# Moving the down-projection weight gradient of a spectral-plus-MLP backward pass out of the MLP into a filler phase

## The chip, the cores and the metric

One core of a Trainium2 chip runs the whole program. The metric is device time in microseconds (us) of one execution. Before the change six executions gave 2395.0 to 2404.82 us, with a median of 2399.89.

## The reference

The reference computes a block and the gradients of all its inputs but B_x: sequence S = 2048, width D = 576, hidden width F = 4608, bfloat16.

```
mod = (silu(c) @ w_mod).reshape(6, D)          # sa, ca, ga, sb, cb, gb
h   = layernorm(x) * (1 + ca) + sa
x   = x + ga * irfft2(rfft2(h) * (w_r + 1j*w_i))
h   = layernorm(x) * (1 + cb) + sb
x   = x + gb * ((h @ w_gate) * (h @ w_up)) @ w_down
out, vjp = jax.vjp(block, A_x, w_r, w_i, w_gate, w_up, w_down, c, w_mod)
return (out, *vjp(grad_out))
```

With hh = (h @ w_gate) * (h @ w_up) and dO = grad_out * gb, the gradient of w_down is hh^T @ dO, a [4608, 576] product over all 2048 rows. It is the product that the change moves.

## The kernel before

The program is written with a tile framework: the code names tiles in pools with a number of buffers, and a list scheduler fixes the order of the instructions on each engine ahead of time, from the order of the code, the data and the free buffers. Each engine then runs its own list in order, and waits on semaphores where it must. A transfer is issued by an engine's queue: most by SP, a few by ACT and POOL.

The 2048 rows are held as 16 blocks of 128 rows (NB = 16; HB = 8 is half of them). The stages, in order:

1. Tables of sines and cosines (build_tables: Fd, FdB, FdT, CF, SF, PT, K), stored to DRAM for the backward pass.
2. The rows of dO = grad_out * gb (tile dO_b), transposed into dOT (pt_b), 16 blocks. Then the spectral weights: load_w_xlayout loads Wn (2048 x 289 twice) and transposes it to Wx (pt_w). Then LayerNorm 1 by rows into h1T.
3. rfft2 as matmuls (ps_d, ps_s1, ps_s2), cmul (product with Wx), irfft2u (ps_s2i, transposes pt_z, ps_s1i, then for each row block ps_y). Each ps_y goes to cons_fwd: ya, x2, LayerNorm 2, h2, and a transpose into h2T, which is stored as one transfer.
4. mlp_phase: two halves (hf = 0, 1) of 1024 rows, and in each nine chunks of 512 columns of F. A chunk loads its weights, computes ps_g, ps_u, ps_d, the products hhT, dgT and duT, the output sum ps_o, the transposes hh_c, dg_c and du_c, the input gradient ps_h, and the weight gradients ps_dwd (line 618, from hh_c and dO_h) and ps_dw (line 628). dw_out stores the weight gradients of half 0 as fp32 partial sums (dWd_p, dWg_p, dWu_p); in half 1 it loads them (dw_f), adds and writes the result (dw_bf). The he rows follow each half (he_row: xn_b and ya_b are loaded by POOL, lb_dx, dya_b); those of half 1 stand after the MLP.
5. Backward transform: Wx again, rfft2 of dyAT, cmul, then the gradient of the spectral weights (cmul_conj_f32 into gWx, store_w_natural with transposes pt_gw into gWn), then irfft2u with cons_bwd for each ps_y: LayerNorm backward on DVE, lb_dx on POOL, and the column sums acc_sa and acc_ca added up on POOL.
6. finals: column sums ps_cs, the row gradients gathered in gm, the gradient of w_mod as five products ow, and that of c.

Of the kernel before, what the change touches and what calls it, by code (L numbers as in the profile page):

```python
# [7 lines left out]
ACT = mybir.ActivationFunctionType  # L8
# [17 lines left out]
class K:  # L26

    def __init__(self, ctx, tc, dbg=None):
        self.ctx = ctx
        self.tc = tc  # L30
        self.nc = tc.nc
        self.dbg = dbg or {}
        self.evac_i = 0
# [80 lines left out]
    def build_tables(self, es=None):  # L114
        nc, tc, ctx = self.nc, self.tc, self.ctx
        self.tpool = (es or ctx).enter_context(tc.tile_pool(name="tables", bufs=1))
# [3 lines left out]
        with tc.tile_pool(name="tgen", bufs=1) as gp, tc.tile_pool(name="tgen2", bufs=2) as gp2:  # L120
# [25 lines left out]
            self.FdB = tpb.tile([128, 5, 2, DF], BF16, name="FdB")  # L146
            nc.vector.tensor_copy(self.FdB[:], self.Fd[:])
            nc.vector.tensor_scalar(self.FdB[:, :, :, 0:1], self.Fd[:, :, :, 0:1], 0.5, None, op0=ALU.mult)
            nc.vector.tensor_scalar(self.FdB[:, :, :, DF - 1:DF], self.Fd[:, :, :, DF - 1:DF], 0.5, None, op0=ALU.mult)
            self.FdT = tpb.tile([128, 3, 2, D], BF16, name="FdT")  # L150
            self.FdTA = tp.tile([128, 3, 2, D], BF16, name="FdTA")
            di = gp.tile([128, D], I32, name="di")
            nc.gpsimd.iota(di[:], pattern=[[1, D]], base=0, channel_multiplier=0)
            d_row = gp.tile([128, D], FP32, name="d_row")
            nc.vector.tensor_copy(d_row[:], di[:])
            kci = gp.tile([128, 3], I32, name="kci")
            for kc, (k0, ksz) in enumerate(KCH):
                nc.gpsimd.iota(kci[:, kc:kc + 1], pattern=[[0, 1]], base=k0, channel_multiplier=1)
            k_col = gp.tile([128, 3], FP32, name="k_col")
            nc.vector.tensor_copy(k_col[:], kci[:])  # L160
            sc0 = gp.tile([128, 3], FP32, name="sc0")
            sc1 = gp.tile([128, 3], FP32, name="sc1")
            nc.vector.tensor_scalar(sc0[:], k_col[:], 0.0, -0.5, op0=ALU.is_equal, op1=ALU.mult)
            nc.vector.tensor_scalar(sc1[:], k_col[:], float(DF - 1), -0.5, op0=ALU.is_equal, op1=ALU.mult)
            nc.vector.tensor_tensor(sc0[:], sc0[:], sc1[:], op=ALU.add)
            nc.vector.tensor_scalar(sc0[:], sc0[:], 1.0, None, op0=ALU.add)
            for kc in range(3):
                idx = gp2.tile([128, D], FP32, tag="idx_fdt", name="idx_fdt")
                nc.vector.tensor_scalar(idx[:], d_row[:], k_col[:, kc:kc + 1], None, op0=ALU.mult)
                self.trig3(gp2, {"cos": self.FdT[:, kc, 0, :], "nsin": self.FdT[:, kc, 1, :]}, idx[:], D, [128, D])  # L170
                nc.vector.tensor_scalar(self.FdTA[:, kc, :, :], self.FdT[:, kc, :, :], sc0[:, kc:kc + 1], None, op0=ALU.mult)
# [11 lines left out]
            idx = gp.tile([128, NB, 128], FP32, name="idx_cf")  # L183
# [3 lines left out]
            self.PT = tp.tile([128, NB, 3, 128], BF16, name="PT")  # L187
            sri = gp.tile([128, NB, 128], I32, name="sri")
            nc.gpsimd.iota(sri[:], pattern=[[1, NB], [NB, 128]], base=0, channel_multiplier=0)
# [289 lines left out]
for _f in (transpose_b, ln_rows, phase0_mod, layernorm_fwd, transpose_sd, rfft2, irfft2u, load_w_xlayout, cmul):  # L479
    setattr(K, _f.__name__, _f)  # L480
# [591 lines left out]
```

## Time and profile before

| | |
|---|---|
| median of six executions | 2399.89 us (2395.0 to 2404.82) |
| the profiled execution's own time | 2402.17 us |
| its span in the profile | 2400.3 us |
| mean granted TensorE clock | 0.868 |
| busy: PE, DVE, ACT, POOL | 1854.4, 1161.5, 764.9, 284.8 us |
| DMA | 262.49 MB in 270574 packets |
| first and last ps_y, forward | 252.9, 328.3 us |
| first ps_g | 361.5 us |
| first and last ps_y, backward | 2234.8, 2319.5 us |

Busy time is a sum over stages. A stage is read by its own stretch: which engine is full in it, which waits, and for whom. In the rows that follow, a group's line gives engine, operation, tiles and shape, count, busy time and the mean of one in ns, then the idle time of the engine ahead of it and what ended that. Rows of the chain give the start in us, the length and what it was. In table rows of a transfer, the last number is the median time from issue to landing in us. L with a number is a line of the kernel before.

### The profile page before, as it was taken

What the parts mean: (1) busy time and instruction counts of PE and PEld (TensorE: products, weight loads), DVE (VectorE), ACT (ScalarE), POOL (GpSimd) and SP (SyncE); (2) the same over time, 40 slices, a digit from 0 to 9 for tenths busy, and PEclk for the clock granted to TensorE, in tenths of its full rate; (3) what the DMA queues carried; (4) which work ended last, traced back from release to release, by engine and by line L of the source; (5) the groups of instructions that cost most, each with busy time, mean ns of one, the idle gap of its engine ahead of it and who ended that gap; (6) DMA issues with size and microseconds to landing.
All of it is one profiled execution on the core that took longest, in us unless ns stands there. A gap on an engine that the chain in (4) does not pass through costs nothing. (4 is left out here: it accounts for less than half of the span.)

```text
span 2400.3 us, 31077 instructions
## 1 busy us (share of the span) xinstructions
PE 1854.4 (77%) x12125; PEld 1142.5 (48%) x12223; DVE 1161.5 (48%) x2125; ACT 764.9 (32%) x1189; POOL 284.8 (12%) x301
## 2 busy tenths in 40 slices
PE   2375749999999999996789999999999961824630
PEld 1253525656566656663446556556555630613420
DVE  7446642234333433342864444434444466294793
ACT  3467524232322332231322211211311310538422
POOL 1100340000000000001430000000000035000670
PEclk7587659999999999997899999999999985965655
DMA  3620373342234224219563253244243055111135
GB/s 121 225 76 41 126 268 84 89 118 76 64 97 116 51 70 118 79 60 299 167 195 77 75 144 92 79 125 106 71 119 99 29 185 195 53 41 40 52 116 137
DMA packets 270574, 262.49 MB, mean 109 GB/s; under 512 B 136806, under 2 KB 222694, under 8 KB 268764
## 3 DMA queue, kind: packets, MB, share of 16 engines
q1 hardware_dynamic: 261580, 237.05, 34.2%
q0 software_dynamic: 4640, 20.65, 2.7%
q10 hardware_dynamic: 4208, 2.81, 0.4%
q8 instruction: 95, 1.56, 0.3%
q14 instruction: 51, 0.42, 0.1%
HBM read 128.45 MB, written 101.33 MB: 96 GB/s over the span
## 5 line engine op out<-in xcount | busy, mean ns | idle before, releaser
L604 PE MATMUL ps_h<-wgT_c,dgT 128*128 128x288 bf16 x1152 | 297.3, 287 | 0.0
L606 PE MATMUL ps_h<-wuT_c,duT 128*128 128x288 bf16 x1152 | 294.5, 287 | 0.0
L628 PEld LDWEIGHTS <-h_h 128*128 128x128 bf16 (+1 forms) x1440 | 142.7, 102 | 224.0 <-issue 79.7
L561 ACT CAST gT<-ps_g 128x512 bf16<-128x512 f32 x144 | 84.4, 586 | 469.0 <-PE ps_g L551 414.4
L551 PE MATMUL ps_g<-h2T_h,wg_c 128*128 128x512 bf16 x683 | 177.0, 384 | 19.4 <-DMA h2T_h<-h2T_s 16.2
L554 PE MATMUL ps_u<-h2T_h,wu_c 128*128 128x512 bf16 x702 | 180.1, 383 | 7.5 <-DVE dw_bf L671 6.6
L628 PE MATMUL ps_dw<-dg_c,h_h 128*128 128x512 bf16 (+1 forms) x702 | 164.4, 390 | 27.0 <-DVE dw_bf L671 18.0
L594 PE MATMUL ps_o<-wd_c,hhT 128*128 128x288 bf16 x1152 | 172.6, 287 | 12.8 <-DVE hhT L575 12.2
L557 PE MATMUL ps_d<-dOT_h,wdT_c 128*128 128x512 bf16 x720 | 179.9, 381 | 3.4 <-DVE dw_bf L671 1.7
L628 PE MATMUL ps_dw<-du_c,h_h 128*128 128x512 bf16 (+1 forms) x702 | 165.6, 385 | 13.7 <-DVE dw_bf L671 8.0
L575 DVE TENSOR_TENSOR hhT<-gT,uT 128x512 bf16<-128x512 bf16 x144 | 62.3, 433 | 230.3 <-ACT uT L562 230.1
L711 ACT COPY dg_c<-pt 128x512 bf16<-128x512 bf16 x144 | 84.4, 586 | 238.1 <-DVE hh_c L710 238.1
L618 PE MATMUL ps_dwd<-dO_h,hh_c 128*128 128x288 bf16 x1152 | 144.4, 286 | 2.3 <-DVE dw_bf L671 2.3
L612 DVE TENSOR_TENSOR dh_acc<-dh_acc,ps_h 128x576 f32<-128x576 f32 x128 | 96.5, 754 | 96.6 <-PE ps_h L606 96.6
L526 POOL MEMSET wg_c<- 64x512 bf16 x18 | 9.3, 519 | 1083.5 <-PE ps_g L551 1003.1
L618 PEld LDWEIGHTS <-hh_c 128*128 128x128 bf16 x1152 | 112.7, 98 | 31.0 <-issue 2.6
L594 PEld LDWEIGHTS <-hhT 128*128 128x128 bf16 x1152 | 108.4, 98 | 37.0 <-DVE hhT L575 13.6
L606 PEld LDWEIGHTS <-duT 128*128 128x128 bf16 x1152 | 113.1, 98 | 25.5
L604 PEld LDWEIGHTS <-dgT 128*128 128x128 bf16 x1152 | 113.3, 98 | 24.7
L671 DVE TENSOR_TENSOR dw_bf<-dw_f,ps_dw 128x512 bf16<-128x512 f32 (+1 forms) x90 | 61.6, 685 | 118.7 <-DMA dw_f<-dWu_p 57.7
L551 PEld LDWEIGHTS <-wg_c 128*128 128x128 bf16 x720 | 69.8, 99 | 98.3 <-issue 15.1
L554 PEld LDWEIGHTS <-wu_c 128*128 128x128 bf16 x720 | 70.9, 99 | 94.6 <-issue 11.9
(362 smaller groups left out, 2965.2 us busy)
## 6 DMA issues: line engine op xcount, KB each, us to landing
wd_c<-in_B_w_down_dram SPq DMA_DIRECT2D x18, 576.0 KB, 4.2
dWd_p<-dw_f SPq DMA_DIRECT2D x36, 288.0 KB, 2.6
dw_f<-dWd_p SPq DMA_DIRECT2D x36, 288.0 KB, 3.3
wg_c<-in_B_w_gate_dram SPq DMA_DIRECT2D x18, 512.0 KB, 3.9
wu_c<-in_B_w_up_dram SPq DMA_DIRECT2D x18, 512.0 KB, 5.0
dWg_p<-dw_f SPq DMA_DIRECT2D x36, 256.0 KB, 2.0
dWu_p<-dw_f SPq DMA_DIRECT2D x36, 256.0 KB, 2.0
dw_f<-dWg_p SPq DMA_DIRECT2D x36, 256.0 KB, 2.8
```

The lines of the kernel that those rows point to most:

```text
L551: nc.tensor.matmul(ps_g[:], wg_c[:, kt, fs], h2T_h[:, kt, cs], start=(kt == 0), stop=(kt == 4))
L554: nc.tensor.matmul(ps_u[:], wu_c[:, kt, fs], h2T_h[:, kt, cs], start=(kt == 0), stop=(kt == 4))
L557: nc.tensor.matmul(ps_d[:], wdT_c[:, kt, fs], dOT_h[:, kt, cs], start=(kt == 0), stop=(kt == 4))
L561: nc.scalar.copy(gT[:], ps_g[:])
L575: nc.vector.tensor_tensor(hhT, v4(gT), v4(uT), op=ALU.mult)
L594: nc.tensor.matmul(ps_o[:, h, :288], (hhTs[ft][:, st, :] if USE_DMA_T else hhTs[ft][:, ss]), wd_c[:, ft, h * 288:(h + 1) * 288], start=(ft ...
L604: nc.tensor.matmul(ps_h[:, h, :288], (dgTs[ft][:, st, :] if USE_DMA_T else dgTs[ft][:, ss]), wgT_c[:, ft, h * 288:(h + 1) * 288], start=(f ...
L606: nc.tensor.matmul(ps_h[:, h, :288], (duTs[ft][:, st, :] if USE_DMA_T else duTs[ft][:, ss]), wuT_c[:, ft, h * 288:(h + 1) * 288], start=Fa ...
L612: nc.vector.tensor_tensor(da, da, ps_h[:, :, :288], op=ALU.add)
L618: nc.tensor.matmul(ps[:, h, :288], hh_c[:, bl, fs], dO_h[:, bl, h * 288:(h + 1) * 288], start=(bl == 0), stop=(bl == HB - 1))
L628: nc.tensor.matmul(ps[:dsz, :], h2_h[:, bl, kt * 128:kt * 128 + dsz], src_c[:, bl, :], start=(bl == 0), stop=(bl == HB - 1))
L711: nc.scalar.copy(dg_c[:, sb * 4:(sb + 1) * 4, fs], pt1[:, 4:8, :])
```

## The change

**The down-projection gradient.** With DEFER_DWD the MLP no longer computes ps_dwd. It stores hh_c to DRAM (hh_s), and after the code of the backward transform dwd_filler computes the gradient in 36 steps of 128 columns of F, each over all 2048 rows, so that there is no partial sum. Its instructions are laid by the scheduler between those of the backward transform, and behind them.

```diff
-                        for ft in range(4):
+                        if DEFER_DWD:
+                            nc.gpsimd.dma_start(scr["hh"][:, hf * HB:(hf + 1) * HB, f0:f0 + FC], hh_c[:])
+                        for ft in (range(0) if DEFER_DWD else range(4)):
                             fs = slice(ft * 128, (ft + 1) * 128)
                             ps = psAcc.tile([128, 2, 512], FP32, tag="acc", name="ps_dwd")
...
+def dwd_filler(self, pool, psum_pool, scr, out_6, dO_all):
+    nc = self.nc
+    for ft in range(F // 128):
+        hh_t = pool.tile([128, NB, 128], BF16, tag="hh_t", name="hh_t")
+        nc.gpsimd.dma_start(hh_t[:], scr["hh"][:, :, ft * 128:(ft + 1) * 128])
+        ps = psum_pool.tile([128, 2, 512], FP32, tag="fill", name="ps_fill")
+        for h in range(2):
+            for b in range(NB):
+                nc.tensor.matmul(ps[:, h, :288], hh_t[:, b, :], dO_all[:, b, h * 288:(h + 1) * 288],
+                                 start=(b == 0), stop=(b == NB - 1))
+        o = pool.tile([128, 2, 288], BF16, tag="dwd_o", name="dwd_o", bufs=1)
+        nc.scalar.copy(o[:], ps[:, :, :288])
+        nc.gpsimd.dma_start(out_6[ft * 128:(ft + 1) * 128, :].rearrange("p (h d) -> p h d", h=2), o[:])
...
+        if DEFER_DWD:
+            fp_ = es.enter_context(tc.tile_pool(name="fillp", bufs=2))
+            dO_all = fp_.tile([128, NB, D], BF16, name="dO_all", bufs=1)
+            nc.gpsimd.dma_start(dO_all[:], scr["dO"])
+            kb.dwd_filler(fp_, kb.psF, scr, out_6, dO_all)
```

On PE, in the first chunk of the MLP, the input gradient ps_h is followed before by ps_dwd (64 matmuls to a chunk):

```order
L604 MATMUL ps_h<-wgT_c,dgT 128x288
L606 LDWEIGHTS duT
L606 MATMUL ps_h<-wuT_c,duT 128x288
L618 LDWEIGHTS hh_c
L618 MATMUL ps_dwd<-dO_h,hh_c 128x288
```

and in the changed kernel, at the same place (its line numbers are its own):

```order
L628 MATMUL ps_h<-wgT_c,dgT 128x288
L630 LDWEIGHTS duT
L630 MATMUL ps_h<-wuT_c,duT 128x288
L654 LDWEIGHTS h_h
L654 MATMUL ps_dw<-dg_c,h_h 128x512
```

The gate's weight gradient ps_dw now follows ps_h at once.

On POOL, at the end of the MLP, the he rows of half 1 begin before with their loads, right behind the memsets of the last chunks:

```order
L526 MEMSET wg_c 64x512
L526 MEMSET wu_c 64x512
L535 MEMSET wdT_c 64x512 x2
L728 DMA xn_b<-xn_s 128x576
L730 DMA ya_b<-ya_s 128x576
L728 DMA xn_b<-xn_s 128x576
```

and now the last stores of hh_c, the load of dO_all and the first two loads of the filler stand ahead of them:

```order
L638 DMA hh_s<-hh_c 128x8x512
L817 MEMSET wdT_c 64x512
L638 DMA hh_s<-hh_c 128x8x512 x2
L1080 DMA dO_all<-dO_s 128x9216
L801 DMA hh_t<-hh_s 128x16x128 x2
L754 DMA xn_b<-xn_s 128x576
L756 DMA ya_b<-ya_s 128x576
```

So three large loads were put ahead of the rows on POOL's queue.

On POOL, at the end of the program, the list ends before with the column sums of cons_bwd and lb_dx:

```order
L692 TENSOR_TENSOR lb_dx<-lb_v,dx_b 128x576
L962 TENSOR_TENSOR acc_sa<-acc_sa,dh_20985 128x576
L965 TENSOR_TENSOR acc_ca<-acc_ca,pr 128x576
L692 TENSOR_TENSOR lb_dx<-lb_v,dx_b 128x576
L965 TENSOR_TENSOR acc_ca<-acc_ca,pr 128x576
L692 TENSOR_TENSOR lb_dx<-lb_v,dx_b 128x576 x2
```

and now with pairs of a filler load and a filler store, 17 loads behind the last lb_dx:

```order
L718 TENSOR_TENSOR lb_dx<-lb_v,dx_b 128x576
L809 DMA out_dram<-dwd_o 128x576
L801 DMA hh_t<-hh_s 128x16x128
L809 DMA out_dram<-dwd_o 128x576
L801 DMA hh_t<-hh_s 128x16x128
L809 DMA out_dram<-dwd_o 128x576
```

The sums acc_sa and acc_ca are gone from POOL, and the filler's transfers stand in the row phase and behind it. On PE the same list puts 784 of the filler's 1152 matmuls behind the last ps_y.

**The backward transform.** rfft2 of dyAT no longer waits for Wx, which is loaded behind it. irfft2u with cons_bwd stands ahead of cmul_conj_f32 and store_w_natural. The column sums acc_sa and acc_ca become two stores per row block (rows_sa, rows_ca), loaded again and summed by 64 matmuls with a vector of ones.

```diff
         kb.rfft2(dyAT, kb.FdB, G)
+        Wx = kb.load_w_xlayout(kb.stg, A_w_r, A_w_i)
         gX = kb.stg.tile([128, 2, NKH, 128], BF16, tag="stg", name="gX")
         kb.cmul(wk, gX, G, Wx, conj_b=True)
+        def cons_bwd(b, ps):
...
+            nc.sync.dma_start(scr["rows_sa"][:, b, :], dh1b[:])
...
+            nc.sync.dma_start(scr["rows_ca"][:, b, :], pr[:])
...
+        kb.irfft2u(gX, kb.FdT, cons_bwd)
...
         kb.cmul_conj_f32(wk, gWx, G, Xl, OSCALE)
         kb.store_w_natural(kb.stg, gWx, out_2, out_3)
```

**The forward stage.** LayerNorm 1 runs inside the table building (mid_hook): x is loaded in two transfers, and all statistics come before one square root. The tables FdB, FdT and PT are built after it. Wx is loaded, and the dO rows are computed, behind rfft2. In cons_fwd two adds go from POOL to DVE, and dO^T and h2^T are stored to DRAM block by block (transpose_b_to_dram) instead of in one transfer each. The PSUM pools are six and two buffers up to the transposes of irfft2u, and are split anew behind them.

```diff
         kb.rfft2(h1T, Fdp, X)
+        Wx = kb.load_w_xlayout(kb.stg, A_w_r, A_w_i)
         nc.sync.dma_start(scr["X"], X[:])
+        for b in range(NB):
...
+            nc.vector.tensor_tensor(dO_b[:], g_b[:], kb.mod[:, 5, :], op=ALU.mult)
+            nc.sync.dma_start(scr["dO"][:, b, :], dO_b[:])
+            kb.transpose_b_to_dram(wk, scr["dOT"], dO_b, b)
...
-            nc.gpsimd.tensor_tensor(x2[:], t[:].rearrange("p h d -> p (h d)"), x_b[:], op=ALU.add)
+            nc.vector.tensor_tensor(x2[:], t[:].rearrange("p h d -> p (h d)"), x_b[:], op=ALU.add)
...
-            nc.gpsimd.tensor_tensor(h2_b[:], h2m[:], kb.mod[:, 3, :], op=ALU.add)
+            nc.vector.tensor_tensor(h2_b[:], h2m[:], kb.mod[:, 3, :], op=ALU.add)
             nc.sync.dma_start(scr["h2"][:, b, :], h2_b[:])
-            kb.transpose_b(h2T, h2_b, b)
+            kb.transpose_b_to_dram(rows2, scr["h2T"], h2_b, b)
```

A second filler in the diff (dhh_filler, under PRE_DHH = False) and the load_wdT that was cut out of the chunk's code don't change what runs.

More of the change, by code (lines that the diff above doesn't have):

```diff
@@ L449, in cmul, with transpose_b_to_dram @@
             nc.vector.tensor_tensor(Oi, t3[:], t4[:], op=ALU.add)
+def transpose_b_to_dram(self, pool, dram_T, src_b, b):
+    nc = self.nc
+    blk = pool.tile([128, 5, 128], BF16, tag="tblk", name="tblk")
+    nc.gpsimd.memset(blk[64:, 4, :], 0.0)
+    pt = self.psT.tile([128, 8, 128], BF16, tag="tr", name="pt_bd")
+    for kt in range(5):
+        dsz = 128 if kt < 4 else 64
+        nc.tensor.transpose(pt[:dsz, kt, :], src_b[:, kt * 128:kt * 128 + dsz], self.ident[:])
+    nc.scalar.copy(blk[:, 0:4, :], pt[:, 0:4, :])
+    nc.scalar.copy(blk[:64, 4, :], pt[:64, 4, :])
+    nc.sync.dma_start(dram_T[:, :, b * 128:(b + 1) * 128], blk[:])
 def transpose_b(self, dst, src_b, b):
@@ L825, in full_kernel @@
     scr = {}
[L826 removed]
+    for nm in ("xn1", "ya", "xn2", "h2", "dO", "dyA", "rows_sa", "rows_ca"):
         scr[nm] = dp.tile([128, NB, D], BF16, name=nm + "_s")
@@ L870, in full_kernel @@
[L870 to L880 removed]
+        kb.tpool = es.enter_context(tc.tile_pool(name="tables", bufs=1))
@@ L969, in full_kernel @@
-        kb.irfft2u(gX, kb.FdT, cons_bwd)
-        for i, a_ in enumerate((acc_sa, acc_ca)):
+        if DEFER_DWD:
[3 more added lines that the diff above has]
+            kb.dwd_filler(fp_, kb.psF, scr, out_6, dO_all)
+        for i, nm in enumerate(("rows_sa", "rows_ca")):
+            rows_t = kb.stg.tile([128, NB, D], BF16, tag="stg", name="rows_t")
+            nc.sync.dma_start(rows_t[:], scr[nm])
```

307 lines of the change are left out of this document (183 added, 124 removed).

## The prediction

> **What bounds the kernel now.** I read the table of stretches first (busy time of each engine per stretch, then the clock that TensorE was granted), because this program has stages with quite different limits.
>
> ```profile
> 250.00:300.00 50.00, 38.80 (x236) 26.14 (x235) 34.68 (x82) 24.51 (x49) 23.72 (x25) 0.70 0.45 152
> ...
> 400.00:1100.00 700.00, 690.98 (x4682) 425.88 (x4723) 255.50 (x514) 210.40 (x357) 15.45 (x29) 1.00 0.32 93
> ...
> 1150.00:1950.00 800.00, 738.30 (x4903) 448.82 (x4944) 381.69 (x711) 178.59 (x303) 54.62 (x67) 0.98 0.40 107
> ...
> 2250.00:2300.00 50.00, 25.48 (x114) 16.18 (x113) 49.77 (x67) 13.46 (x20) 39.83 (x24) 0.57 0.32 92
> ```
>
> The columns after the length are PE, PEld, DVE, ACT and POOL. In the first half of the MLP (400 to 1100) PE is busy 691 of 700 us at full clock, so any matmul taken out there comes off the time. In the second half it is 738 of 800. In the rows of the backward transform (2250 to 2300) DVE is full and PE half idle. Next, the same table for the instructions of tile ps_dwd alone (PE, DVE, ACT), over one chunk of the first half and one of the second:
>
> ```profile
> 442.00:523.00 81.00, 8.00 (x64) 1.51 (x2) 1.28 (x2) 1.00 0.31 86
> ...
> 1308.30:1395.40 87.10, 7.98 (x66) 3.02 (x4) 0.00 (x0) 1.00 0.38 101
> ```
>
> Then the chain that ended last, for a chunk of the second half, the seam after the MLP, and the end:
>
> ```profile
> 1308.29 3.93 PE ps_dwd L618 x32
> ...
> 1315.10 3.54 DMA dw_f<-dWd_p
> ...
> 1395.41 3.93 PE ps_dwd L618 x32
> ...
> 2018.41 1.98 POOL dya_b L764
> 2022.95 15.13 DMA Wn<-in_A_w_i_dram
> 2038.16 6.36 DMA Wn<-in_A_w_r_dram
> ...
> 2155.37 4.64 ACT gWn L40
> ...
> 2182.03 7.18 ACT gWn L40 x2
> ...
> 2330.83 1.88 POOL lb_dx L692
> ...
> 2392.07 3.17 ACT ow L995
> ```
>
> A second-half chunk takes 87.1 us, and the fp32 partial sums (dw_f) are waited for in each. The transform waits for its weights (Wn), then its output gradient (gWn) runs ahead of the rows, and nothing but the small final products follows the last row.
>
> **Term 1, the MLP.** The 1152 matmuls ps_dwd leave a stage that PE bounds: 8.00 us per chunk, 9 chunks per half, so 72 us in the first half. In the second half each chunk also loses the load of a partial sum, 3.54 us in the chain. The next load (dWg) follows on the same SP queue and would move into part of that wait, so I take half of it: 9 x (8.0 + 1.8) = 88. Bounds: 72 + 72 = 144 and 72 + 9 x 11.5 = 176; I take 160. New in the chunk is one store of hh_c, 1 MB in 1024 rows, issued by POOL. What hides it: POOL's first memset of each chunk waits for PE for tens of microseconds.
>
> ```profile
> L526 POOL MEMSET wg_c<- 64x512 bf16 x18 | 9.3, 519 | 1083.5 <-PE ps_g L551 1003.1 <-PE ps_u L554 80.4
> ```
>
> Its 18 MB stand against 72 transfers of 288 KB that go. If POOL were held longer than that idle time, 60 us a chunk, the weights' memsets and with them ps_g would be late.
>
> **Term 2, the forward stage.** Groups by line, with the idle time before them and its cause:
>
> ```profile
> L457 PE MATMUL pt_b<-ident,dO_b 128*128 128x128 bf16 (+1 forms) x80 | 13.5, 309 | 26.7 <-DVE dO_b L865 26.1 <-ACT dOT L40 0.6
> L551 PE MATMUL ps_g<-h2T_h,wg_c 128*128 128x512 bf16 x683 | 177.0, 384 | 19.4 <-DMA h2T_h<-h2T_s 16.2 <-ACT gT L561 0.8 <-issue 0.2
> L907 POOL TENSOR_TENSOR x<-x2t,x_b 128x576 f32<-128x576 f32 x16 | 21.4, 1338 | 96.7 <-DVE x2t L903 91.2 <-DVE ln_rstd L472 5.0 <-DVE ln_nmr L474 0.4
> ```
>
> The dO rows stand ahead of LayerNorm 1 and hold PE 13.5 + 26.7 = 40 us. Behind rfft2 they run beside the multiplication by the weights: gain 40. The store of h2T per row lets the first MLP half load when eight rows are done, where PE now waits 16: gain 16. Against it, Wx is now loaded after rfft2, ahead of the product; the two loads of Wn took 15.13 + 6.36 = 21.5 us at the seam, and I charge them whole. Sum 35. Bounds: 56 if that load hides under rfft2, 0 if the dO rows only delay the product on DVE and ACT. The two adds moved from POOL to DVE cost DVE two operations per row and save a hand-over (1.34 us each for x); POOL there mostly waits for DVE, so I set this to nothing (at most 16 x 1.3 = 21 us either way). The order of table building is costed at nothing: DVE covers it now too.
>
> **Term 3, what POOL must issue.** Each hh_t load has 2048 rows of 256 B (512 KB). No POOL transfer of before has over 128 rows. POOL's issues, and landing times:
>
> ```profile
> L103 POOL DMA_DIRECT2D tab_SF<-SF x1 | 1.3, 1346 | 4.4 <-ACT SF L73 4.4
> L518 POOL DMA_DIRECT2D h_h<-h_s x2 | 1.2, 576 | 2.6 <-PE ps_y L398 2.6
> L103 POOL DMA_DIRECT2D tab_CF<-CF x1 | 0.5, 531 | 1.1 <-ACT CF L79 1.1
> L103 POOL DMA_DIRECT2D tab_Kr<-Kr x1 | 0.5, 542 | 0.4 <-DVE Kr L221 0.4
> ...
> Wn<-in_A_w_r_dram SPq DMA_DIRECT2D x2, 1156.0 KB, 7.4
> xn_b<-xn_s POOLq DMA_DIRECT2D x16, 144.0 KB, 3.4
> ```
>
> 32 KB (tab_Kr) and 1152 KB (h_h) cost the same 0.54 to 0.58 us, so bytes are free and rows are the question. Call the issue time G. Lower bound: rows free, 0.57. Upper bound: all of 0.55 us goes with its 128 rows, 16 x 0.55 = 8.8. Nothing says how the 0.55 splits; I take 3, near the middle of the two as a ratio. Landing after the issue: between 3.4 (128 rows) and 7.4 (Wn's 2048 rows of 578 B); with 256 B rows I take 4.5.
>
> The Trainium skill (DMA: Bandwidth & Descriptors, Anatomy of one DMA) says that one can emit a lot of descriptors before the added cost shows. By it G would stay at the lower bound and the sum would be the 2235 of the second rival; no run here shows it yet.
>
> **Term 4, the seam.** By the changed order POOL issues dO_all (0.6) and two hh_t ahead of the first xn_b and ya_b of the second half's rows, and those rows start the chain that ended at 2020.4 (2018.41 + 1.98). That is 0.6 + 2 x 3 = 7 us later (bounds 2 and 18). The rows end at 2020.4 - 160 - 35 + 7 = 1832.
>
> **Term 5, to the rows of irfft2.** Groups and tile view (durations, then first and last start):
>
> ```profile
> L398 PE MATMUL ps_y<-FdT_r,ZT x192: 282/447/448, 2234.8 to 2319.5; 96*128 96x288 bf16 x128, 97*128 97x288 bf16 x64
> ...
> L807 PE MATMUL pt_gw<-ident,gWx 128*128 128x128 bf16 x74 | 9.8, 307 | 56.1 <-ACT gWn L40 32.3 <-ACT gWx L789 23.9
> L40 ACT COPY dw_f<-ps_dwd 128x576 f32<-128x576 f32 x24 | 15.3, 639 | 109.6 <-PE ps_dwd L618 76.4 <-DMA dWd_p<-dw_f 33.2
> ```
>
> Now it is 2234.8 - 2020.4 = 214 us from the end of the rows to the first ps_y. The Wn load (21.5) now passes beside rfft2, and the gWn stretch (2155.4 to 2189.2, 34 us) comes after the rows: 159 remain. PE has seven of 36 filler steps there, where it idles anyway. First ps_y at 1991, last 85 us later as now (DVE bound it; POOL loses acc_sa and acc_ca and gains some nine loads), 2076.
>
> **Term 6, the tail.** By the changed order 784 of 1152 filler matmuls (24.5 of 36 steps) stand behind the last ps_y. One step: load, 32 matmuls, one ACT copy, one store. Matmuls take 32 x 0.125 = 4.0 us at full clock, 5.7 at the 0.70 of the stretch 250 to 300, whose PE share is near what I expect here. With two hh_t buffers a step takes (G + 4.5 + 5.7 + 0.6) / 2 = 6.9 at G = 3; with the single PSUM buffer, matmuls and the copy (0.64) in turn with half a microsecond of hand-overs, 5.7 + 0.64 + 0.5 = 6.9 too. The first 7.2 steps lie among the transposes pt_gw, which took 9.8 + 56.1 = 66 us alone; the steps alone need 50; I take 58, since DVE starts that product beside the rows. The other 17.3 take 119. Last copy, store and landing: 5. End: 2076 + 58 + 119 + 5 = 2258. The final products have their own path: from the last lb_dx (2332.7) to the end at 2400.3 is 68 us; the changed order puts the last column sums nine steps before the end, at 2191, so they end at 2259, level with the filler. I take 2258.
>
> The profiled execution took 2402.17, 1.9 above its span, and the median is 2.3 below that. So 2258 + 1.9 - 2.3: **2258**.
>
> **Rivals.** First, POOL pays by the row, G = 8.8. The step is then (8.8 + 4.5 + 5.7 + 0.6) / 2 = 9.8, the rows end at 1844, last ps_y 2088, and 24.5 x 9.8 + 5 gives 2333. For it: no row shows that rows are free. Against: h_h has 36 times the bytes of tab_Kr for the same price, so bytes at least cost POOL nothing.
>
> Second, rows are free. The step is 4.0 + 0.64 + 0.5 = 5.1 and the filler would end at 2221, but then the final products bind: last column sums at 2071 + 58 + 8.3 x 5.1 = 2171, and 68 more, some 2235 to 2240.
>
> Third, the forward stage gains nothing (the zero bound of term 2): 2293.
>
> Fourth, slower. POOL's loads are serial, two ahead of the rows and the rest through two buffers, so in G the end is about 2205 + 14.25 G (2 G at the seam, 12.25 G in the tail); from G = 13.7 us on the change loses. It needs more than a price by the row: tab_SF took 1346 ns where tab_CF with the same 128 rows took 531, a factor 2.5 while DVE was busy. With 8.8 x 2.5 = 22 us beside a busy DVE, the seam costs 45, the filler among the rows 4.5 x 22, the next 7.2 steps 158, the last 17.3 at 9.8 us 170: 1870 + 159 + 99 + 158 + 170 + 5 = 2461. Against it: h_h, ya_b and most others stay at 0.53 to 0.58.
>
> The Trainium skill (SBUF — State Buffer, Who interferes with whom and the box on DVE blocking DMA) says that a POOL-issued transfer can't have its descriptors written while DVE runs in a two-port mode. The spread of tab_SF agrees with such a hold, and it is why this case has a chance at all.
>
> **Chances.** The measurement tells a change from none at about 0.2%, 5 us. Likeliest case (G from 1 to 6) 0.50; price by the row 0.17; rows free 0.13; forward gain lost 0.08; slower 0.09; gains and losses that happen to cancel 0.03. Faster 0.88, same 0.03, slower 0.09. Range: the low end is rows free with the Wn load hidden and term 1 at its upper bound, 2237 - 21 - 16 = 2200. The high end is the price by the row, 2333, and half of the forward gain lost, 2350.
>
> **What would show it.** Right: no ps_dwd and no dWd partials in the MLP, chunks of 73 and some 77 us; ps_g starting near 327; hh_t issues of about 3 us on POOL; the last ps_y near 2076; the chain ending in ps_fill and dwd_o at steps of 6.9 us. Wrong: hh_t at 0.6 or above 8; the chain at the end in ow and gm instead of the filler; the second half's chunk unchanged beyond 8 us, with dWg waiting where dWd did; PE waiting for Wn ahead of the forward product for over 22 us; PE stopped by a filler matmul ahead of rfft2 or of a ps_y, which the static order allows if a load is late.

## The result, and the profile after

The changed kernel took 2269.76 us (median of 8 executions, 2264.19 to 2274.18) against 2399.91 us before: a ratio of 0.9454, 95% interval 0.9441 to 0.9467. The forecast was 2258, in a range from 2200 to 2350. The sum came out within 12 us, but several of its terms were off by more, in both directions, and the experiments tell why.

The changed kernel by stretches, cut at the end of the first chunk, of the last chunk of each half, of the he rows, and at the first and the last ps_y (columns as above: PE, PEld, DVE, ACT, POOL busy, granted clock, DMA share, GB/s):

```profile
402.60:1011.30 608.70, 592.90 (x3900) 351.91 (x3938) 242.70 (x493) 180.24 (x308) 22.99 (x37) 0.99 0.35 98
1141.20:1774.90 633.70, 596.11 (x3896) 352.26 (x3933) 277.95 (x540) 150.05 (x256) 20.86 (x31) 0.99 0.37 102
1774.90:1847.60 72.70, 22.85 (x81) 11.68 (x81) 68.13 (x95) 11.88 (x16) 49.33 (x40) 0.57 0.55 176
1847.60:1982.40 134.80, 112.34 (x874) 81.35 (x879) 61.23 (x84) 82.26 (x125) 14.48 (x18) 0.89 0.35 101
1982.40:2051.60 69.20, 54.85 (x405) 41.07 (x403) 64.25 (x126) 36.53 (x60) 25.83 (x20) 0.93 0.74 229
2051.60:2267.30 215.70, 135.50 (x906) 96.60 (x903) 70.91 (x78) 72.00 (x56) 47.60 (x53) 0.81 0.63 164
```

The last row is the tail: 216 us behind the last ps_y, with no engine full. PE is busy 135 us of it, and the DMA engines are 63% busy. The same cuts give the same stages in other kernels; this table holds their lengths in us, worked out from the starts and ends in each trace (the sums are the spans). "No deferral" and "no filler" are experiments told below, and so is "three edits", the fastest kernel of this study.

| stage | before | changed | no deferral | no filler | three edits |
|---|---|---|---|---|---|
| to the end of the first MLP chunk | 450.6 | 402.6 | 409.8 | 403.0 | 405.7 |
| from there to the end of the he rows | 1569.6 | 1445.0 | 1570.1 | 1443.1 | 1450.7 |
| to the first ps_y | 214.5 | 134.8 | 122.9 | 126.4 | 134.4 |
| first to last ps_y | 85.1 | 69.2 | 64.5 | 69.7 | 70.2 |
| last ps_y to the end | 80.5 | 215.7 | 152.1 | 148.2 | 194.8 |
| span | 2400.3 | 2267.3 | 2319.4 | 2190.4 | 2255.8 |

Ahead of the tail the kernels of this study differ by more than their edits explain. The first chunk ends between 402.6 and 411.2 us in those kernels with the deferral whose code is the same up to there, and with the same forward code and a filler the last backward ps_y ends between 2051.6 (the changed kernel) and 2067.3. The cause is open. So an edit of the tail is read below by the length of the tail as well as by the whole time.

The tile views of ps_y, hh_t and hh_s (durations in ns: least, median, most, then the first and last start); G, the price that the forecast could not read, stands in the last two:

```profile
L405 PE MATMUL ps_y<-FdT_r,ZT x192: 282/284/448, 1982.4 to 2051.3; 96*128 96x288 bf16 x128, 97*128 97x288 bf16 x64
L801 POOL DMA_DIRECT2D hh_t<-hh_s x36: 1148/1166/1217, 1749.6 to 2232.2; - x36
L638 POOL DMA_DIRECT2D hh_s<-hh_c x18: 885/885/952, 377.4 to 1743.4; - x18
```

and its landing in the part on DMA issues of the page:

```profile
hh_t<-hh_s POOLq DMA_DIRECT2D x36, 512.0 KB, 5.8
```

An issue of 2048 rows takes 1.17 us, one of 1024 rows 0.89, and one of 128 rows 0.56 as before: sixteen times the rows for twice the price. Landing takes 5.8 us. The waits of the tail, by engine, line and what was waited for (us in total, times, longest):

```profile
POOL hh_t L801 <- PE ps_fill L805: 110.3, 21, 16.7
ACT dwd_o L808 <- DMA out_dram<-dwd_o: 81.6, 14, 16.0
PE ps_fill L805 <- ACT dwd_o L808: 50.8, 20, 16.5
...
PEld L805 <- DMA hh_t<-hh_s: 32.6, 9, 15.5
```

POOL is not what the filler waits for; POOL waits for the matmuls. The largest wait that feeds the matmuls is ACT's: with one buffer, the copy dwd_o waits until the store of the step before has landed. The loads of hh_t hold PE another 32.6 us. A step without such waits takes 4.1 us of matmuls and 0.64 of copy; the 24.5 steps took 8.6 on the mean.

The longest of ACT's waits, 16.0 us, is a case of its own. These are two stores on SP's queue and, 24 us later, the copy that waited:

```profile
2232.96 0.43 SPq L1127 DMA_DIRECT2D out_dram<-gcb  x1
2233.44 1.60 SPq L1128 DMA_DIRECT2D out_dram<-gcb  x1
2256.59 0.64 ACT L808 CAST dwd_o<-ps_fill 128x576 bf16<-128x576 f32 x1 [15.95 <-DMA out_dram<-dwd_o]
```

The store of dwd_o that the copy waits for was issued at 2235.3, 2 us behind the two stores of gcb. Those hold the gradient of c, 1.1 KB, which the trace shows as 576 packets of 2 bytes. Before the change it is the fourth store of ow that is issued next behind them, and it takes 12.7 us where each of the three before it takes 3.5; without the deferral and without the filler it takes 13.3 and 14.3. No run changed the form of that store, so that it holds up the transfers around it is read from the order in time and not shown by an experiment.

### The profile page after: what moved, and what is told of

It reads as the page before. It is cut to its first block, busy times and chain, and to the rows that moved or that the text cites. A ratio compares the mean times of both kernels' runs of the same rounds, so it can differ in the third digit from the quotient of the medians.

```text
span 2267.3 us, 31129 instructions
## 1 busy us (share of the span) xinstructions
PE 1848.4 (82%) x12179; PEld 1143.4 (50%) x12279; DVE 1092.9 (48%) x2043; ACT 778.0 (34%) x1225; POOL 268.0 (12%) x343
## 4 chain that ended last, share of the span: by engine, by line
PE 25%; issue 9%; DMA 7%; DVE 5%; POOL 2%; ACT 2%; SPq 1%; DVEq 0%; POOLq 0%; ACTq 0%
PE ps_d L577 3%; PE ps_u L573 3%; PE ps_h L628 3%; PE ps_h L630 3%; PE ps_o L618 3%; PE ps_g L570 3%; DMA dw_f<-dWg_p 2%; DMA dw_f<-dWu_p 2%; PE ps_dw L654 2%; DVE dw_bf L697 1%; ACT T L41 1%; PE pt L740 1%; PE ps_fill L805 1%; POOL hh_t L801 1%; DVE lb_junk L708 1%
## 5 line engine op out<-in xcount | busy, mean ns | idle before, releaser
L805 PE MATMUL ps_fill<-dO_all,hh_t 128*128 128x288 bf16 x1152 | 184.9, 320 | 57.2 <-ACT dwd_o L808 56.9
L805 PEld LDWEIGHTS <-hh_t 128*128 128x128 bf16 x1152 | 124.0, 109 | 106.0 <-DMA hh_t<-hh_s 34.8
L654 PE MATMUL ps_dw<-dg_c,h_h 128*128 128x512 bf16 (+1 forms) x702 | 156.9, 380 | 1.0
L697 DVE TENSOR_TENSOR dw_bf<-dw_f,ps_dw 128x512 bf16<-128x512 f32 (+1 forms) x90 | 61.1, 684 | 134.8 <-DMA dw_f<-dWg_p 68.9
L577 PEld LDWEIGHTS <-wdT_c 128*128 128x128 bf16 x720 | 70.6, 98 | 91.7 <-DMA wdT_c<-in_B_w_down_dram 5.9
```

The costliest lines, as they stand in the source:

```text
L577: nc.tensor.matmul(ps_d[:], wdT_c[:, kt, fs], dOT_h[:, kt, cs], start=(kt == 0), stop=(kt == 4))
L654: nc.tensor.matmul(ps[:dsz, :], h2_h[:, bl, kt * 128:kt * 128 + dsz], src_c[:, bl, :], start=(bl == 0), stop=(bl == HB - 1))
L697: nc.vector.tensor_tensor(o[:np_], t[:np_], ps, op=ALU.add)
L805: nc.tensor.matmul(ps[:, h, :288], hh_t[:, b, :], dO_all[:, b, h * 288:(h + 1) * 288], start=(b == 0), stop=(b == NB - 1))
```

## The experiments

**Which part of the change earns what.** The first kernel puts the gradient back into the MLP:

```diff
-DEFER_DWD = True
+DEFER_DWD = False
```

> The changed kernel with the down-projection gradient back in the MLP (ps_dwd and its partial sums as before), all the rest of the change kept. Theory A: the restructuring of the forward stage (40 us, read at the end of the first MLP chunk less ps_dwd), of the seam to the first ps_y (80 us) and of the rows (16 us) makes the gain, and the deferral gives back in the tail what it takes out of the MLP: about 2400 - 136 + 10 = 2275 us, within 15 of the changed kernel. Rival B: the deferral carries the gain, since its 140 us in the MLP are only partly paid back: 2320 us or more.

It took 2323.69 us, ratio 0.9666 (0.9632 to 0.9699). Rival B is right: without the deferral the change gains 3.3%, with it 5.5%. The table tells why theory A failed. The restructuring saves 41 us up to the first chunk, 92 to the first ps_y and 21 in the rows, near the 40, 80 and 16 that I had read; but 72 us of it come back behind the last ps_y, since the gradient of the spectral weights (gWn) now stands there and the final products behind it. Tile view of gWn on ACT in this kernel:

```profile
L41 ACT COPY gWn<-pt_gw x7: 2857/4478/4566, 2168.9 to 2245.4; 128x1024 bf16<-128x1024 bf16 x5, 128x640 bf16<-128x640 bf16 x2
```

and the chain behind it:

```profile
2249.04 7.07 DMA gmod_s<-row
2257.02 9.96 DMA gmod_s<-row
2267.04 6.85 DMA gm<-gmod_s
2273.91 3.19 ACT ow L1111
...
2297.45 13.28 DMA out_dram<-ow
```

From the last gWn to the end it is transfers that wait for each other: two column sums stored as one row each (7 and 10 us), gm loaded, and five products with one buffer, each behind the store of the last. The deferral takes 7 + 125 = 132 us out of the MLP and the forward end of it, and gives back 12 ahead of the first ps_y, 5 in the rows and 64 in the tail: 52 net.

The second kernel keeps the deferral and leaves the filler out:

```diff
-            kb.dwd_filler(fp_, kb.psF, scr, out_6, dO_all)
```

> The changed kernel without the filler: hh_c is stored as before, but the gradient of w_down is neither computed nor written. Theory A: the last chunk of the MLP loses 8 us to the filler's first three loads (dWg landed in 11 us there instead of 3), and fills cost some 10 us ahead of the first ps_y: rows end near 1840, first ps_y near 1962, end near 2110. The eight chunks of the first half still take 75 us, not 74. Rival B: the last chunk is slow for a reason of its own (its dWg wait stays at 11 us, rows end at 1847), and the filler in front of the first ps_y is free (135 us from the rows' end).

It took 2193.16 us, ratio 0.9123 (0.9096 to 0.915), far over the 2110 that I gave. Two readings go the way of theory A: the last chunk, 83.7 us with the filler, takes 79.3, which is half of the 8 us that it gave, and the first ps_y comes 8 us sooner after the rows. But the rows end at 1846.1, where rival B had them, and with no filler in it the tail still takes 148 us, and its chain is the same as without the deferral:

```profile
2098.14 4.49 ACT gWn L41
...
2109.29 4.50 DVE gWn L46
...
2118.10 7.47 DMA gmod_s<-row
...
2126.47 10.30 DMA gmod_s<-row
...
2136.86 7.60 DMA gm<-gmod_s
2144.48 3.19 ACT ow L1110
2147.68 3.49 DMA out_dram<-ow
...
2167.97 14.28 DMA out_dram<-ow
```

So the tail has two chains: gWn, column sums and final products, 148 us by themselves; and the filler. Of the first, the 68 us from the column sums to the end are as I had priced them (2122.2 to 2190.4 here). The stretch from the last ps_y to the last gWn, which I had put at 58, takes 75 with no filler in it.

**Which of the two chains ends the changed kernel.** The second buffer for the copy takes the largest wait from the filler's chain:

```diff
-        o = pool.tile([128, 2, 288], BF16, tag="dwd_o", name="dwd_o", bufs=1)
+        o = pool.tile([128, 2, 288], BF16, tag="dwd_o", name="dwd_o", bufs=2)
...
-            row = wk.tile([128, D], FP32, tag="row", name="row", bufs=1)
+            row = wk.tile([128, D], FP32, tag="dh1", name="row")
```

> The changed kernel with two buffers for dwd_o (the small tile row shares the buffers of dh1, which makes the room). Theory A: the tail is set by the ACT copy that waits for the landing of the store before (81.6 us of waiting behind the last ps_y); with a second buffer a step is bound by 4.1 us of matmuls, the copy and the hand-overs, 5.6 us, and the end comes 35 to 55 us earlier: 2215 to 2235 us. Rival B: the landing of hh_t (5.8 us, two buffers) or the final products take its place at once: 2255 us or more.

It took 2278.16 us, ratio 0.9465 (0.9426 to 0.9504): no gain that can be told from the changed kernel. The filler itself did gain. Tile views of ow and of ps_fill in the changed kernel, and then in this one:

```profile
L1111 ACT ACTIVATE ow<-gm,cs_col x5: 3175/3176/3178, 2214.6 to 2257.9; 128x3456 bf16<-128x3456 f32 x4, 64x3456 bf16<-64x3456 f32 x1
L805 PE MATMUL ps_fill<-dO_all,hh_t x1152: 282/286/448, 1849.4 to 2262.4; 128*128 128x288 bf16 x192
```

```profile
L1111 ACT ACTIVATE ow<-gm,cs_col x5: 3174/3175/3179, 2234.2 to 2270.2; 128x3456 bf16<-128x3456 f32 x4, 64x3456 bf16<-64x3456 f32 x1
L805 PE MATMUL ps_fill<-dO_all,hh_t x1152: 282/286/448, 1856.6 to 2243.3; 128*128 128x288 bf16 x192
```

From the last ps_y to the last ps_fill it was 211 us and is 181: the waits were worth 30. The one beside gcb alone had been 16, and here the filler is done before gcb is issued (2252). But the last product ow, which started level with the filler's last matmul in the changed kernel (2257.9 and 2262.4), now starts 27 us behind it. It starts 12 us later than it did, and 11 of them had been lost ahead of the tail, whose length is the same: 215.2 us for 215.7. Rival B holds in its second half: the final products take the filler's place at once.

**Making the filler faster still.** Three buffers for dwd_o, and one PSUM bank for each half of a step:

```diff
-        ps = psum_pool.tile([128, 2, 512], FP32, tag="fill", name="ps_fill")
+        o = pool.tile([128, 2, 288], BF16, tag="dwd_o", name="dwd_o", bufs=3)
         for h in range(2):
+            ps = psum_pool.tile([128, 512], FP32, tag="fill", name="ps_fill", bufs=2)
             for b in range(NB):
-                nc.tensor.matmul(ps[:, h, :288], hh_t[:, b, :], dO_all[:, b, h * 288:(h + 1) * 288],
+                nc.tensor.matmul(ps[:, :288], hh_t[:, b, :], dO_all[:, b, h * 288:(h + 1) * 288],
...
+            nc.scalar.copy(o[:, h, :], ps[:, :288])
```

> The changed kernel with three buffers for dwd_o and the filler's PSUM tile split into two tiles of one bank each, so that a half is copied while the other half's matmuls run. Theory A (store landing first, then the single PSUM tile): a step comes down to 4.1 us of matmuls and the load's chain (1.2 + 5.8 + 4.1 + 0.6) / 2 = 5.9 us, tail 24.5 x 5.9 = 145 instead of 216: 2195 to 2215 us, 10 to 20 below the kernel with only a second dwd_o. Rival B: the final products bind once the filler is faster, and both kernels end alike near 2225.

It took 2293.91 us, ratio 0.9533 (0.95 to 0.9566), by the ratios some 19 us slower than the changed kernel; both expectations missed. Of the 25 us between the two profiled executions, 16 were lost ahead of the tail; the tail itself is 225.0 us for 215.7. The filler ended earliest of all, at 2227.8, but the last product ow started at 2284.2. The chain holds, behind the filler:

```profile
2230.82 9.94 DMA gmod_s<-row
2240.83 7.67 DMA gm<-gmod_s
2272.04 12.08 DMA out_dram<-ow
```

The column sums end at 2230.0, behind the whole filler: the scheduler placed them among its steps on PE, and an order that is fixed ahead of time keeps them there.

**Putting the column sums first.** The code of rows_t, ps_cs and row goes ahead of the gradient of the spectral weights, with one dwd_o buffer and with two:

```diff
         kb.irfft2u(gX, kb.FdT, cons_bwd)
+        for i, nm in enumerate(("rows_sa", "rows_ca")):
+            rows_t = kb.stg.tile([128, NB, D], BF16, tag="stg", name="rows_t")
...
         Xl = kb.stg.tile([128, 2, NKH, 128], BF16, tag="stg", name="Xl")
```

> The changed kernel with the code of the column sums (rows_t, ps_cs, row) put ahead of the gradient of the spectral weights, one dwd_o buffer as in the change. Theory C (two paths end level in the changed kernel: the filler at 2262.7 and the final products at 2261.1, so that taking one away alone gives little): the filler's end stays, 2255 to 2270 us. Rival D (the final products alone set the end of the changed kernel, as they do in the kernel with two dwd_o): 2245 us or less.

> The column sums put first and two dwd_o buffers together. Theory C (both paths have to be shortened): the column sums end some 60 us earlier, gm is loaded behind the last gWn, the final products end near 2220, and the filler near 2240: 2235 to 2250 us, though either edit alone gave under 10 us. Rival D (the second dwd_o gives nothing whatever the final products do, since the load chain of hh_t sets the step): 2260 us or more.

They took 2297.4 us (ratio 0.9564, 0.9534 to 0.9594) and 2292.44 (0.954, 0.951 to 0.9571). The edit costs over 20 us, and the tail is 244.7 and 229.3 us. Both theories of the first kernel missed; of the second, rival D's number holds (2260 or more), but not its reason, since a further kernel below, with a faster load of hh_t, still ends at 2278 us. The column sums did move, from 2178 to 2096 and 2104. But rows_t and Xl take turns in the same pool (stg), so that now Xl waits for the column sums (it is loaded at 2090 in the first kernel instead of 1999) and the first gWn starts at 2113 instead of 2052; gm is loaded only behind the stores of gWn (2193 instead of 2196), so that the last product ow starts at 2260 as before (2258). What they then do to the filler, in the second of these kernels:

```profile
ACT ow L1111 <- DMA out_dram<-ow: 23.3, 3, 16.8
```

ACT runs its list in order, and a product ow that waits 16.8 us for the store of the last one holds up the copy dwd_o behind it. (That store was issued 0.4 us ahead of those of gcb.) A second buffer for ow, on top of the two edits:

```diff
-            ow = wk.tile([128, 6 * D], BF16, tag="ow", name="ow", bufs=1)
+            ow = wk.tile([128, 6 * D], BF16, tag="ow", name="ow", bufs=2)
```

> As the kernel before, with two buffers for ow as well, so that a product need not wait for the store of the last one. Theory C: the final products are off the path by then, so 0 to 5 us less than with one ow. Rival E (the ACT products between the dwd_o copies still hold up the filler while they wait for a store): 8 us less or more.

It took 2286.79 us, ratio 0.9506 (0.9468 to 0.9544). The difference of 6 us is inside the intervals, so theory C and rival E are not told apart; the five products ow came down from 62 to 31 us in the profile.

**The rows of the load.** The same stage order as the second of the two kernels above, with hh_s laid out by step:

```diff
-                            nc.gpsimd.dma_start(scr["hh"][:, hf * HB:(hf + 1) * HB, f0:f0 + FC], hh_c[:])
+                            for ft in range(4):
+                                nc.gpsimd.dma_start(scr["hh"][:, cch * 4 + ft, hf * HB:(hf + 1) * HB, :], hh_c[:, :, ft * 128:(ft + 1) * 128])
...
-        nc.gpsimd.dma_start(hh_t[:], scr["hh"][:, :, ft * 128:(ft + 1) * 128])
+        nc.gpsimd.dma_start(hh_t[:], scr["hh"][:, ft, :, :])
...
-    scr["hh"] = dp.tile([128, NB, F], BF16, name="hh_s")
+    scr["hh"] = dp.tile([128, F // 128, NB, 128], BF16, name="hh_s")
```

> The column sums first, two dwd_o buffers, and hh_s laid out so that an hh_t load has 128 rows of 4 KB instead of 2048 of 256 B; the price is four stores of 1024 short rows per chunk in the MLP instead of one. By the rows so far (0.56 us at 128 rows, 0.89 at 1024, 1.17 at 2048) the issue of hh_t comes down to 0.56. Theory F (the load's chain sets a step of the filler, 1.2 + 5.8 + 4.1 over two buffers): landing falls from 5.8 to some 4 us, the step from 5.2 to 4.9, 5 to 10 us less than without it. Rival G (matmuls, copy and hand-overs through the single PSUM tile set the step): no change within 5 us, and the MLP is up to 5 us longer.

It took 2278.32 us, ratio 0.9482 (0.9455 to 0.9509), 14 us less than without it. The two profiled executions differ by 18 us. Of these, 8 lie ahead of the end of the first chunk, where the edit changes only the stores of one chunk; 7 lie in the tail (222.1 for 229.3) and 3 in the last chunk (81.4 for 84.1). So theory F holds, with about the 5 to 10 us that it gave. Groups on POOL in this kernel:

```profile
L639 POOL DMA_DIRECT2D hh_s<-hh_c x72 | 64.0, 889 | 187.6 <-DVE hh_c L737 184.5 <-DVE dgT L600 1.7 <-DVE duT L601 1.4
L802 POOL DMA_DIRECT2D hh_t<-hh_s x36 | 19.4, 539 | 217.1 <-PE ps_fill L806 209.5 <-PE pt_b L477 7.6
```

A store of 1024 rows of 256 B costs POOL 0.889 us, as much as one of 1024 rows of 1 KB: here rows have a price and bytes none. The median landing of hh_t came down from 5.8 to 4.3 us.

**All that helped, in the changed kernel's own order.** Two buffers for dwd_o, two for ow, and the layout by step:

> The changed kernel with its own order of the stages, two dwd_o buffers, two ow buffers and the hh_s layout that makes an hh_t load 128 rows. Theory C (the end is the later of filler and final products, and each holds the other up through ACT's fixed order: with two dwd_o alone the filler ended at 2243.6 and the final products at 2273; two ow shortened these from 62 to 31 us): filler near 2235, products near 2250, 2245 to 2262 us, the fastest so far. Rival N (the column sums slide later whenever the filler gets faster, since PE's fixed order gives it the room, so that the final products start later by what they gained): 2265 us or more.

It took 2256.8 us, ratio 0.9386 (0.9363 to 0.9408), below the interval of the changed kernel (0.9441 to 0.9467): the fastest of the study. Its chain in the tail:

```profile
2176.15 0.73 PE ps_cs L1089 x6
2176.92 4.08 PE ps_fill L806 x32
...
2196.62 13.32 DMA gmod_s<-row
2210.01 10.76 DMA gm<-gmod_s
2220.86 3.78 DVE junkw L1115 x2
```

and one of its last stores, in the list of DMA issues:

```profile
out_dram<-gcb SPq DMA_DIRECT2D x1, 0.1 KB, 14.1
```

Against the changed kernel the tail is 21 us shorter (194.8 for 215.7), while 9 us were lost ahead of it. Many steps of the filler now follow each other at 4.9 us. The number is theory C's, but rival N's mechanism is there too: the column sums, spread between filler steps on PE, end 135 us behind the last ps_y instead of 127, and the final products behind them set the end. The last of these is the gradient of c: gcb is issued at 2240.7 and lands 14.1 us later, at 2254.8 of 2255.8. A kernel that puts the column sums early without giving gWn's buffers away was not tried.

**Single terms.** The store of hh_c left out, as well as the filler (this kernel and the two that follow ran once each):

```diff
-                            nc.gpsimd.dma_start(scr["hh"][:, hf * HB:(hf + 1) * HB, f0:f0 + FC], hh_c[:])
+                            pass
```

> The changed kernel without the filler and without the store of hh_c (the gradient of w_down is not computed). It tells where 1.2 us of the 8.0 of each chunk of the first MLP half went. Theory H (the 1 MB store shares the DMA engines with the stores of partial sums and the weights): the chunks of the first half take 74.0 us instead of 75.3 and those of the second 77 to 78 instead of 78.9. Rival I (the partial sums' stores are too slow for a shorter chunk by themselves): 75.3 and 78.9 stay.

It took 2188.99 us. The first half's chunks took 74.4 to 76.2 us as with the store (74.2 to 76.2), the second's 78.3 on the mean instead of 79.0. Rival I: the store costs under 1 us a chunk. What a shorter chunk may run into is seen in the copies of the partial sums on ACT, before and after the change (busy, mean | idle, cause):

```profile
L40 ACT COPY dw_f<-ps_dw 128x512 f32<-128x512 f32 (+1 forms) x60 | 35.1, 584 | 122.9 <-PE ps_dw L628 47.7 <-DMA dWg_p<-dw_f 37.9 <-DMA dWd_p<-dw_f 25.2
```

```profile
L41 ACT COPY dw_f<-ps_dw 128x512 f32<-128x512 f32 (+1 forms) x60 | 35.1, 584 | 188.4 <-DMA dWg_p<-dw_f 90.9 <-PE ps_dw L654 68.3 <-DMA dWu_p<-dw_f 24.8
```

They wait 91 us for the stores of dWg_p and 25 for those of dWu_p. Before they waited 38 and 25 for those of dWg_p and dWd_p, and the copies of ps_dwd, which are gone, another 33 (their line is in the prediction). So by the causes that the lines list the waits for stores grew from 96 to 116 us: two buffers serve the remaining stores, and the time that ps_dwd gave them between is gone. A third buffer was not tried, so this is the likely cause and not a shown one.

The sums acc_sa and acc_ca put back on POOL, in the kernel without the deferral (the adds are those of the kernel before):

```diff
-            nc.sync.dma_start(scr["rows_sa"][:, b, :], dh1b[:])
...
+                nc.gpsimd.tensor_tensor(acc_sa[:], acc_sa[:], dh1[:], op=ALU.add)
...
+                nc.gpsimd.tensor_tensor(acc_ca[:], acc_ca[:], pr[:], op=ALU.add)
```

> The changed kernel without the deferral and with acc_sa and acc_ca added up on POOL again, as before the change, instead of stores and matmuls with ones. Theory J (POOL's adds slow the DVE operations beside them: lb_u takes 1.95 us in the kernel before and 0.81 in the changed one): the 16 rows from first to last ps_y take 80 to 85 us again instead of 65, with lb_u near 1.9. Rival K (the rows were faster because of the order of the stages): 65 us stay.

It took 2364.89 us, and 86 us from first to last ps_y instead of 64.5. Theory J holds. The same operation in the rows of the kernel before and of the changed one, and then of this kernel and of the one without the deferral, which differs from it in these sums alone:

```profile
L686 DVE SCALAR_TENSOR_TENSOR lb_u<-xn_b,lb_nm,lb_dxn 128x576 f32<-128x576 bf16 x13 | 23.6, 1812 | 0.0
```

```profile
L712 DVE SCALAR_TENSOR_TENSOR lb_u<-xn_b,lb_nm,lb_dxn 128x576 f32<-128x576 bf16 x12 | 9.7, 806 | 0.0
```

```profile
L712 DVE SCALAR_TENSOR_TENSOR lb_u<-xn_b,lb_nm,lb_dxn 128x576 f32<-128x576 bf16 x11 | 17.4, 1584 | 0.0
```

```profile
L712 DVE SCALAR_TENSOR_TENSOR lb_u<-xn_b,lb_nm,lb_dxn 128x576 f32<-128x576 bf16 x12 | 9.7, 808 | 0.1
```

POOL computes lb_dx in all four, so none is free of POOL's adds: in the rows POOL is busy 67 of 85 us before and 26 of 69 in the changed kernel.

The Trainium skill (SBUF — State Buffer, Who interferes with whom) says that a DVE instruction with two SBUF inputs contends with a GpSimd instruction that reads SBUF. lb_u has two such inputs, and 1584 ns beside the two added sums against 808 without them agrees.

The dO rows put back ahead of LayerNorm 1:

```diff
+        for b in range(NB):
+            g_b = wk.tile([128, D], BF16, tag="g_b", name="g_b")
...
         def ln1_block():
```

> The changed kernel with the 16 dO rows put back ahead of LayerNorm 1. Theory L (they held PE and DVE for 40 us there): the first ps_y of the forward stage comes 25 to 40 us later than 229, and so does the end. Rival M (in the changed order DVE is full with tables there and the rows fill gaps of PE and ACT): under 15 us later; the 40 us of the forward stage then come from the batched LayerNorm and the tables moved behind it.

It took 2286.26 us, but the first ps_y of the forward stage came at 236.9 instead of 229.0. Kernels of this study with the forward code of the changed kernel had it between 228.4 and 236.2, so the move is worth 8 us at most: rival M. The other 9 us by which its span is longer lie behind the first chunk, where the code is the same.

## Why the prediction was right, and where its terms were not

**Term 1, the MLP: 160 forecast, 132 found** (7 + 125, no deferral against the changed kernel). A chunk of the first half lost some 7 us, not 8.0, probably because the copies of partial sums wait longer for their buffers (that cause is argued above, not shown). The second half's chunk came to 78.6 us from 87.3, 8.7 less, not 9.8: dWg's load moved into more of the gap than the half I gave it (DVE's longest wait for it rose from 2.5 to 6.5 us, and that for dWd had been 6.1). The last chunk lost next to nothing (84.3 to 83.7): the filler's first loads, put ahead of the rows on POOL, ran beside its partial sums,

```profile
1751.62 11.03 DMA dw_f<-dWg_p
```

and took back 4 us of it by the experiment without the filler. That kernel keeps the load of dO_all, and there the same load of dWg still took 7.5 us, where the chunks before it took under 3: dO_all may have its share in this too. I had priced those three loads by POOL's issue time alone and not by the DMA engines they share.

**Term 2, the forward stage: 35 forecast, 41 found** at the end of the first chunk (no deferral against before). (The other kernel without the deferral, with the sums back on POOL, gives 37.) The sum held, its parts did not. The first ps_g starts at 301, 61 us sooner than before (361.5), and not at some 327; but the first chunk then takes 109 us without the deferral instead of 89, and why was not taken apart. Moving the dO rows is worth 8 at most, not 40. The Wn load charged with 21.5 is hidden: in the changed kernel the group

```profile
L427 PE MATMUL pt_w<-ident,Wn 128*128 128x128 bf16 x148 | 11.9, 224 | 3.1 <-ACT Wx L41 2.0 <-DVE Wx L46 0.8 <-DMA Wn<-in_A_w_r_dram 0.2
```

waits 0.2 us for it. The ps_y rows, costed at nothing, took 57 us instead of 76. How much of the rest is the batched LayerNorm and how much the tables was not taken apart.

**Term 3, G: 3 forecast, 1.17 found**, between the bounds of 0.57 and 8.8 and near the lower one. The Trainium skill (DMA: Bandwidth & Descriptors, Anatomy of one DMA) has it that many descriptors can be emitted before the cost shows: 1.17 against 0.56 us for sixteen times the rows agrees. The hold that the fourth rival feared did not come: hh_t took at most 1.217 us an issue, in the rows too, with DVE busy 64 of 69 us. That such a hold exists is seen in the table stage, where one store of a table of unchanged size took this before the change and after:

```profile
52.07 0.58 POOL L103 DMA_DIRECT2D tab_FdT<-FdT  x1 [6.49 <-ACT FdT L79]
```

```profile
87.94 1.51 POOL L104 DMA_DIRECT2D tab_FdT<-FdT  x1 [17.78 <-ACT FdT L80]
```

In the second case a DVE tensor_scalar of 1.22 us ran beside it and ended 0.12 us ahead of the end of the issue. The other table stores that took 0.8 to 1.5 us end 0.12 us behind a DVE tensor_scalar, copy or cast as well, in both kernels; tab_CF beside a scalar_tensor_tensor before the change took 0.53. In the backward rows most of DVE's time is scalar_tensor_tensor and tensor_tensor.

**Term 5, to the first ps_y and the rows: 159 and 85 forecast, 135 and 69 found.** I took off the Wn load and the stretch of gWn but not the product ahead of it on DVE (cf_t), which now runs beside the rows and behind them: 24 us too much. In the rows I kept DVE's time although POOL lost the adds that slowed it: 16 too much.

**Term 6, the tail: 182 forecast, 216 found.** Three steps of the working failed.

The stretch from the last ps_y to the last gWn was put at 58 us and took 81 (2051.6 to 2133.0); with no filler in it, it takes 75. I had it from the 66 us of the transposes, less what DVE would do of the product beside the rows. But 32 of the product's 48 operations stood behind the last ps_y. These 23 us are the same work that term 5 left ahead of the first ps_y.

The filler's steps behind that stretch were put at 119 us and took 130. Matmuls ran at 4.1 us a step, not 5.7, and G was smaller, so they should have been shorter. But I counted the landing of a store once, at the end, though dwd_o has one buffer and every copy waits for the landing before it: the second buffer took 30 us off.

The final products were put at 68 us behind the column sums. They take 68 in the kernel without the filler, and beside the filler they took 89 (2178.5 to 2267.3). The store of the second column sum took 16 us instead of 10 until gm could be loaded, and ACT came to the first product 12 us after gm had landed. That filler and products would end level came true (2262.7 and 2261.1), by errors of one sign.

The sum came out because the errors cancel: 21 us too much gain in terms 1 and 4 together and 34 too little time in term 6, against 6 too little gain in term 2 and 40 too much time in term 5. Some 24 of this had to cancel, since it is one product counted on the wrong side of the rows; the rest is luck. Of the rivals, the second named the right wait: with a faster filler the final products bind, as the kernel with two dwd_o showed.

## What to carry to other kernels

Work moved off a full engine into a tail is worth what the tail's own chains leave free: before pricing it, follow each chain there to the end without the moved work, because here they took 148 us with no filler at all. A loop of load, matmul, copy and store can need a second buffer on the store's side as well as on the load's (30 us here), and where two chains end level, shortening one alone gave nothing here. Look also at what is issued just ahead of a store that the chain waits for: a store of 1.1 KB in single elements, or a large load on the same queue, stood there in the worst waits of this tail. Where engines run fixed orders, a small final product placed between long-lived steps holds them up and is held up by them, so moving its code can cost more than its buffers save.

## What the runs showed of the hardware

Outside the table stage, the price of a POOL-issued transfer went with its rows and not with its bytes: 0.53 to 0.59 us at 128 rows (144 KB to 2.3 MB), 0.885 at 1024 rows of 1 KB, 0.889 at 1024 rows of 256 B, and 1.17 at 2048 rows; some 0.3 to 0.4 ns a row. In the table stage, stores of no more rows took up to 1.51 us beside DVE's tensor_scalar, copy and cast. The same 512 KB landed in 5.8 us as 2048 rows of 256 B and in 4.3 as 128 rows of 4 KB (medians, beside other traffic). The second of the two stores of one row of 2304 B (gmod_s) took 5.6 us before the change until the load of gm could go on, and 10 to 16 in the changed kernel, without the deferral, without the filler and with three edits. In these four it was issued 0.8 to 1 us behind the load of wm, 3456 KB on the same queue, and before the change 7 us behind it. The two stores and the load of gm were 25 of the 148 us of the tail without the filler. The second store of gcb, which together with the first is 576 elements of 2 bytes, landed 14 us after its issue before the change and in the kernel with three edits.
